# A block-causal attention with a gated MLP on one core: written order in the first slots, weight pieces spread over ten slots, and the softmax sums inverted later

## The chip, the cores and the metric

The kernel runs on one core of a Trainium2 chip. The metric is the device time of one execution in microseconds. Three runs of the kernel before gave 811.85, 812.12 and 814.16 us, so its time is the median, 812.12 us. The engines are PE (TensorE matmul), PEld (its weight loads), DVE (VectorE), ACT (ScalarE), POOL (GpSimd) and SP (which issues DMAs).

## What is computed

```python
scores = scale * np.matmul(q, k.transpose(0, 1, 3, 2))      # 8 batches, 8 heads, S = 576, D = 64, fp32
scores = np.where(block_i >= block_j, scores, -1000000000.0)  # blocks of 64 positions
attn = np.exp(scores - np.max(scores, axis=-1, keepdims=True))
attn = attn / (np.sum(attn, axis=-1, keepdims=True) + 1e-09)
x = np.matmul(attn, v)                                       # heads laid side by side: (8, 576, 512)
h = x @ w_in                                                 # 512 x 1024, float64 in memory
h = 0.5 * h * (1.0 + np.tanh(c * (h + 0.044715 * h ** 3)))
u, v = h[..., :512], h[..., 512:]
v_n = (v - mu) / np.sqrt(var + 1e-06) * g_ln                 # over the 512 features
v_s = np.einsum('ts,bsd->btd', w_sg, v_n) + b_sg[None, :, None]
out = x + (u * v_s) @ w_out                                  # w_out float64 in memory
```

## The kernel before

Every fp32 product is made of three matmuls: each operand is split into a high part (a cast, `xh`, `kh`, `wi_h`) and a low part (a subtraction, `xl`, `kl`, `wi_l`), and high x high, high x low and low x high are summed in PSUM.

The work is cut into 32 **slots** of one pair of heads each, four slots to a batch (`slot`, L647). A slot makes the softmax sums' inverse (`inverse`, L370: DVE writes `r` from `sums` and inverts it, POOL copies it wide into `rx`), transposes the unnormalised probabilities of its own pair in three parts (`turn`, tiles `pA`, `pB`, `pC`, copied to `ptA`, `ptB`, `ptC` by DVE for one head or by ACT for the other), transposes `rx` into the tiles `pd` and `pe` (`turn_sums`), and multiplies with v (`products`, tile `ob`; `normalise` writes `x` and stores it to `spill`). In between it makes the next pair's scores (`first` and `second`, tile `s`), on which DVE finds the ten maxima (L303) and ACT the exponentials (L316). `split_qk` (L96, POOL) splits q and k of the pair after that.

A batch's **feed-forward** is a queue of groups that are put into holes of the slots of the following batch: 5 v groups (`accv`, a copy by ACT, gelu, and the layer norm as `side` work: moments, `rs`, `centre` on DVE, `scale` L517 to L531 with `vv` on POOL, `vh` on DVE, `vl` on POOL), 8 u groups (`accu`), 8 o groups of the batch before it (`acco`, residual page `xr` loaded from `spill`, summed by DVE and stored as `out_T`), and 8 s groups (`accs`, which need all of `vh` and `vl`). `PLAN` says how many groups stand in each of a slot's four holes: "1112" for the first slot of a batch, "2114" for the other three. So slot 4k holds v, 4k+1 u, 4k+2 o and 4k+3 s; the first batch has no o before it, so its s groups already stand in slot 6.

**Weights.** w_in and w_out are float64 and are converted in pieces of 256 columns (`from_f64`, L170): ACT's absolute value, three DVE operations, ACT's cast (`wi_h`), POOL's subtraction (`wi_l`). Spatial weights w_sgT are split by ACT and POOL (`ws_h`, `ws_l`; the last page with a bias row). `WS` says how many pieces a slot converts: 2, 2, 2, 2, 8, 2, 2, 2, 4, 4; `need` (L256) converts at once what is missing when a part begins.

**What sets the order.** Only PE runs in the order in which the program is written (`PIN = "P"`, L50). On DVE, ACT, POOL and SP a scheduler orders the instructions at build time; in each queue they then run one after the other.

**Buffers.** Pages of one tag share a fixed number of buffers (L57). Tag "r" has two: they hold the residual pages `xr` and also the small tile `r` of `inverse` (L372, the same tag). u, gh, gl and the weight pages have twelve.

Of the kernel before, what the change touches and what calls it, by code (L numbers as in the profile page):

```python
# [20 lines left out]
def kernel(  # L21
# [12 lines left out]
    nc = tc.nc  # L34
# [15 lines left out]
    PIN = "P"  # L50
# [17 lines left out]
    def pin(ins, e):  # L68
        return tc.keep_in_program_order(ins) if e in PIN else ins

    def mm(*a, **k):
        return pin(nc.tensor.matmul(*a, **k), "P")  # L72

    def turn(out, in_):
        return pin(nc.tensor.transpose(out, in_, ident), "P")  # L75
# [20 lines left out]
    def split_qk(n):  # L96
        out = []
        for x, t in zip(raw.pop(n), "qk"):
            hi = sp.tile([P, S], F32R, tag=t + "h", name=t + "h", bufs=1)
            lo = sp.tile([P, S], F32R, tag=t + "l", name=t + "l", bufs=1)  # L100
            if n == 0:
                copy("v" if t == "q" else "a", hi, x)
                nc.vector.tensor_tensor(lo, x, hi.bitcast(F32), op=ALU.subtract)
            else:
                copy("g", hi, x)
                nc.gpsimd.tensor_tensor(lo, x, hi.bitcast(F32), op=ALU.subtract)  # L106
# [19 lines left out]
    t = bank("warm")  # L126
    for _ in range(18):
        nc.tensor.transpose(t[:, :P], ident, ident)
# [3 lines left out]
    nc.gpsimd.memset(mask, 0.0)  # L132
    nc.gpsimd.memset(mask[:BLK, MW - BLK :], -8.0e9)
    half = cp.tile([P, NT], F32, name="half")
    nc.gpsimd.memset(half, -0.5)
    stats = cp.tile([P, NT, 2], F32, name="stats")
    nc.gpsimd.memset(stats, 1.0)


    for s in (0, 1):  # L140
        t = cp.tile([P, NT, 2 * D], F32, name=f"v_f{s}")
        nc.gpsimd.memset(t[TAIL:, NT - 1, :], 0.0)
        v_bufs.append(t)
# [22 lines left out]
    def split_weight(x, dh, dl):  # L166
        nc.scalar.copy(dh, x)
        nc.gpsimd.tensor_tensor(dl, x, dh.bitcast(F32), op=ALU.subtract)

    def from_f64(raw, dh, dl):  # L170
# [4 lines left out]
        tm = page(U32, 2 * n, "w")  # L175
# [14 lines left out]
    def load_weight(src, cols, dh, dl):  # L190

        W = 256
        parts = [(c, slice(f, f + W)) for c in range(NC) for f in range(cols.start, cols.stop, W)]
        raws = {}

        def fetch(k):
            if k < len(parts):
                c, fs = parts[k]
                raws[k] = page(src.dtype, W, "w")
                nc.sync.dma_start(raws[k], src[c * P : (c + 1) * P, fs])  # L200

        for k in range(2):
            fetch(k)
        for k, (c, fs) in enumerate(parts):
            fetch(k + 2)
# [3 lines left out]
            else:  # L209
                from_f64(*args)  # L210
            yield True

    def load_spatial():
        nc.sync.dma_start(g_bc, g_ln.unsqueeze(0).broadcast_to([P, DH]))
        t = page(F32, S, "w")
        nc.gpsimd.memset(t[BLK:, :DH], 1.0)
        nc.vector.tensor_copy(vone[BLK:, :], t[BLK:, :DH])
        for j in range(NT - 1):
            t = page(F32, S, "w")
# [5 lines left out]
        t = page(F32, S, "w")  # L225
        for hf in (0, 1):
            nc.sync.dma_start(t[hf * BLK : (hf + 1) * BLK, :], w_sgT[j * P : S, :])
        t2 = page(F32, S, "w")
        nc.gpsimd.memset(t2[BLK:, :], 0.0)
        nc.sync.dma_start(t2[BLK : BLK + 1, :], b_sg.unsqueeze(0))  # L230
        nc.sync.dma_start(t2[96:97, :], b_sg.unsqueeze(0))
        nc.scalar.copy(ws_h[:, j, :], t)
        nc.gpsimd.tensor_tensor(
            ws_l[:BLK, j, :], t[:BLK, :], ws_h[:BLK, j, :].bitcast(F32), op=ALU.subtract
        )
        nc.scalar.copy(ws_l[BLK:, j, :], t2[BLK:, :])
        nc.vector.tensor_tensor(
# [9 lines left out]
            ("o", load_weight(w_out, slice(0, DM), wo_h, wo_l)),  # L247
# [15 lines left out]
    xs = {}  # L263

    class Scores:


        def __init__(self, n):
            self.qh, self.ql, self.kh, self.kl = qk.pop(n)
            self.sm = sp.tile([P, NT, 2], F32, tag="sums", name="sums", bufs=3)  # L270
            nc.gpsimd.memset(self.sm[:, 0, :], 1.0)
# [27 lines left out]
        def maximum(self, a, i, lo, hi):  # L299
# [3 lines left out]
            nc.vector.tensor_tensor_reduce(  # L303
# [10 lines left out]
        def exponent(self, a, i):  # L314
            r, e = slice(0, QN[i]), EXT[i]
            nc.scalar.activation(  # L316
# [33 lines left out]
    class Values:  # L350
# [19 lines left out]
        def inverse(self):  # L370

            r = sp.tile([P, NT * 2], F32, tag="r", name="r", bufs=2)  # L372
            nc.vector.tensor_scalar_add(r, self.sm.rearrange("p i a -> p (i a)"), 1e-9)
            nc.vector.reciprocal(r, r)
            self.rx = sp.tile([P, NT, 2 * D], F32, tag="rx", name="rx", bufs=1)
            nc.gpsimd.tensor_copy(
# [4 lines left out]
        def turn_sums(self):  # L381
# [4 lines left out]
            t, t2 = bank("pd"), bank("pe")  # L386
            for a in (0, 1):
# [42 lines left out]
        def split(self):  # L430
# [7 lines left out]
            nc.gpsimd.tensor_tensor(lo, x, hi[:, :S].bitcast(F32), op=ALU.subtract)
# [34 lines left out]
    def v_part(b, vv, vn, vn_t, u, g_s):  # L473
        need("v")
        x_s = xs[b]
        for st in range(NT):
# [13 lines left out]
            if st < NT - 1:  # L490
                last = nc.scalar.copy(x, acc).ins
            else:
                vt = sp.tile([P, DH], F32, tag="pt", name="vt", bufs=6)
                nc.scalar.copy(vt[:TAIL, :], acc[BLK:, :])
                nc.vector.tensor_tensor(x, acc[:TAIL, :], vt[:TAIL, :], op=ALU.add)
# [3 lines left out]
        def moments(st):  # L499
# [4 lines left out]
            nc.vector.bn_aggr(stats[:rows, st, :], bs[:rows, :])  # L504
# [8 lines left out]
        def inverse_std():  # L513
            nc.gpsimd.tensor_scalar(rs, stats[:, :, 1], 1e-6, None, op0=ALU.add)
            nc.gpsimd.tensor_tensor(rs, rs, half, op=ALU.pow)

        def scale(st):  # L517
# [6 lines left out]
            if st < NT - 1:  # L524
                hi, lo = vn[st] = page(F32R, DH, "vh"), page(F32R, DH, "vl")
                nc.vector.tensor_copy(hi, x)  # L526
                nc.gpsimd.tensor_tensor(lo, x, hi.bitcast(F32), op=ALU.subtract)  # L527
# [16 lines left out]
    def u_part(b, vv, vn, vn_t, u, g_s):  # L544
        need("u")
        x_s = xs.pop(b)
        for fo in range(NC):
            u.append(page(F32, S, "u"))
            fs = slice(fo * P, (fo + 1) * P)
            for th in (0, 1):  # L550
# [12 lines left out]
                last = nc.scalar.copy(u[fo][:, ts], acc[:, :SH]).ins  # L563
# [192 lines left out]
```

## Time and profile before

| what | value |
|---|---|
| median of 3 runs | 812.12 us (811.85 to 814.16) |
| the profiled execution | 813.77 us, span 812.0 us, mean granted clock 0.968 |
| PE busy | 761.3 us (94%), 7090 instructions |
| DVE, ACT, POOL busy | 480.9, 411.4, 397.0 us |
| chain that ended last, by engine | PE 86%, DVE 5%, POOL 3%, DMA 2% |
| longest wait of PE | 14.5 us, `accs` for `vh` |

The span is the time from the first to the last instruction. A row of the trace gives the start, the length, the engine, the line, the operation and its tiles, and in brackets the idle time before it and what ended that. The chain of waits is followed back from the last instruction: at each step to what released it.

### The profile page before, as it was taken

To read this page: it belongs to the slowest core of one execution; us is meant where nothing else is said; L and a number is where in the kernel's file an instruction comes from. 1 tells how busy PE (TensorE), PEld (TensorE's weight loads), DVE (VectorE), ACT (ScalarE), POOL (GpSimd) and SP (SyncE) were. 2 spreads that over 40 slices of the span, in tenths; PEclk is the share of its full clock that TensorE was granted. 3 is DMA by queue.
4 is the path that set the end of the run, shared out by engine and by line. 5 is a ranking of instruction groups with operands and counts; after the bars stand their busy time and mean duration, and the time that the engine had idled before them with its cause. 6 is when DMAs were issued, how large, how long until landed. Compare 5 with 4: busy or idle time off the path is not lost.

```text
span 812.0 us, 18284 instructions
## 1 busy us (share of the span) xinstructions
PE 761.3 (94%) x7090; PEld 714.0 (88%) x7090; DVE 480.9 (59%) x1477; ACT 411.4 (51%) x1061; POOL 397.0 (49%) x457
## 2 busy tenths in 40 slices
PE   4588993699999999999999999999999999999997
PEld 4467893598999989999999989999899989999997
DVE  6975448277596635854486644865477644952542
ACT  5575585056764357533764347624674337630500
POOL 4664338464467522854358423764348423742341
PEclk8699997599999999999999999999999999999999
DMA  7323225023234112321134112321133211320032
GB/s 242 111 87 89 63 73 153 0 72 99 60 104 132 49 41 79 101 88 57 60 89 137 43 57 60 119 87 59 61 89 113 64 36 56 102 88 16 1 117 88
DMA packets 46922, 65.84 MB, mean 81 GB/s; under 512 B 4082, under 2 KB 22514, under 8 KB 46836
## 3 DMA queue, kind: packets, MB, share of 16 engines
q1 hardware_dynamic: 46836, 64.67, 25.8%
q8 instruction: 56, 0.92, 0.5%
q14 instruction: 30, 0.25, 0.1%
HBM read 45.78 MB, written 18.87 MB: 80 GB/s over the span
## 4 chain that ended last, share of the span: by engine, by line
PE 86%; DVE 5%; POOL 3%; DMA 2%; issue 2%; ACT 1%; DVEq 0%; SPq 0%; POOLq 0%
PE accs L72 15%; PE accv L72 13%; PE accu L72 13%; PE acco L72 12%; PE ob L72 10%; PE s L72 10%; PE pC L75 4%; PE pB L75 4%; PE pA L75 3%; PE pd L75 2%; DVE prob L303 1%; DVE w L181 1%; ACT prob L316 1%; PE pe L75 1%; DVE w L182 1%
## 5 line engine op out<-in xcount | busy, mean ns | idle before, releaser
L316 ACT ACTIVATE prob<-prob,negm 128x576 f32<-128x576 f32 (+3 forms) x320 | 176.8, 554 | 86.5 <-DVE negm L303 83.5
L303 DVE CUSTOM_DVE_ANT_0 prob<-s,mask 128x288 f32<-128x288 f32 (+3 forms) x320 | 121.8, 424 | 61.8 <-PE s L72 61.1
L72 PE MATMUL accs<-ws_h,vh 128*128 128x288 f32 x256 | 79.8, 312 | 16.5 <-DVE vh L526 16.5
L596 POOL TENSOR_TENSOR gl<-u,gh 128x288 fp32r<-128x288 f32 x64 | 52.1, 817 | 64.5 <-DVE gh L595 64.2
L435 POOL TENSOR_TENSOR xh<-x,xh 128x64 fp32r<-128x64 f32 x32 | 14.0, 438 | 140.0 <-DVE xh L434 137.6
L72 PE MATMUL accs<-ws_h,vl 128*128 128x288 f32 x256 | 77.5, 303 | 2.8 <-POOL vl L527 2.8
L72 PE MATMUL accu<-xh,wi_h 128*128 128x288 f32 x256 | 78.1, 305 | 0.0
L72 PE MATMUL acco<-gh,wo_h 128*128 128x288 f32 x256 | 77.8, 304 | 0.0
L72 PE MATMUL accs<-ws_l,vh 128*128 128x288 f32 x256 | 76.5, 299 | 0.0
L72 PE MATMUL accu<-xl,wi_h 128*128 128x288 f32 x256 | 75.4, 295 | 0.0
L72 PE MATMUL acco<-gh,wo_l 128*128 128x288 f32 x256 | 75.4, 295 | 0.0
L72 PE MATMUL accu<-xh,wi_l 128*128 128x288 f32 x256 | 75.4, 295 | 0.0
L72 PE MATMUL acco<-gl,wo_h 128*128 128x288 f32 x256 | 75.4, 294 | 0.0
L594 DVE TENSOR_TENSOR u<-accs,u 128x288 f32<-128x288 f32 x64 | 29.3, 458 | 63.9 <-PE accs L72 63.2
L72 PE MATMUL accv<-wi_h,xh 128*128 128x512 f32 x160 | 65.8, 411 | 0.0
L72 PEld LDWEIGHTS accs<-ws_h,vh 128*128 128x128 f32 x256 | 49.1, 192 | 18.9 <-DVE vh L526 15.7
L72 PE MATMUL s<-kh,qh 64*128 64x288 f32 (+4 forms) x384 | 63.3, 324 | 0.0
L72 PE MATMUL accv<-wi_l,xh 128*128 128x512 f32 x160 | 63.2, 395 | 0.0
L79 POOL CAST kh<-k_f 128x576 fp32r<-128x576 f32 x31 | 21.1, 681 | 84.1 <-PE s L72 79.5
L72 PE MATMUL s<-kh,ql 64*128 64x288 f32 (+4 forms) x384 | 59.6, 305 | 0.8 <-POOL ql L106 0.8
L316 ACT ACTIVATION_READ_ACCUMULATOR prob<-prob,negm 128x1 f32 x320 | 59.8, 187 | 0.0
L72 PE MATMUL s<-kl,qh 64*128 64x288 f32 (+4 forms) x384 | 58.4, 302 | 0.0
(118 smaller groups left out, 2163.7 us busy)
## 6 DMA issues: line engine op xcount, KB each, us to landing
q_f<-in_qT SPq DMA_DIRECT2D x32, 288.0 KB, 3.0
k_f<-in_kT SPq DMA_DIRECT2D x32, 288.0 KB, 2.8
spill<-x SPq DMA_DIRECT2D x32, 288.0 KB, 2.7
xr<-spill SPq DMA_DIRECT2D x32, 288.0 KB, 2.9
out_T<-xr SPq DMA_DIRECT2D x32, 288.0 KB, 2.1
v_f<-in_v SPq DMA_DIRECT2D x32, 256.0 KB, 3.0
w<-in_w_in SPq DMA_DIRECT2D x16, 256.0 KB, 4.7
w<-in_w_out SPq DMA_DIRECT2D x8, 256.0 KB, 3.2
```

The lines of the kernel that those rows point to most:

```text
L72: return pin(nc.tensor.matmul(*a, **k), "P")
L75: return pin(nc.tensor.transpose(out, in_, ident), "P")
L79: return f(dst, src)
L181: nc.vector.tensor_scalar(t, lo, 29, None, op0=ALU.logical_shift_right)
L182: nc.vector.scalar_tensor_tensor(t, hi, 0x80000000, t, op0=ALU.bitwise_and, op1=ALU.bitwise_or)
L303: nc.vector.tensor_tensor_reduce(prob[a][i][r, lo:hi], self.where[a, i, lo], mask[r, MW - (hi - lo) :] if 0 < i and hi == e else mask[r, : ...
L316: nc.scalar.activation(prob[a][i][r, :e], prob[a][i][r, :e], AF.Exp, bias=self.negm[a][r, i : i + 1], scale=-1.0, accum_out=self.sm[r, i, ...
L435: nc.gpsimd.tensor_tensor(hi[:, S:], x[:, S - TAIL :], hi[:, S - TAIL : S].bitcast(F32), op=ALU.subtract)
L594: nc.vector.tensor_tensor(x, acc[:, :SH], x, op=ALU.mult)
L596: nc.gpsimd.tensor_tensor(glo[:, ts], x, ghi[:, ts].bitcast(F32), op=ALU.subtract)
```

## The change

- All four engines run in written order while slots 0 to 3 are issued (`written`); from slot 4 on again only PE. The operations that may be pinned go through a wrapper, so their line in the profile is that of the wrapper.
- The four first slots convert two w_in pieces each, after the sums' transposes, taken column block by column block; the remaining pieces stand at the end of slots 4, 6, 7, 8 and 9, from slot 4 on behind the last maximum on DVE and the last exponential on ACT (`issue_after`).
- Spatial and w_out pages move from the tag with twelve buffers to tag "r" with two; w_out pieces are no longer loaded two ahead.
- `inverse` moves, in all 32 slots, from the slot's start to behind turn B.
- The first batch's groups follow `FIRST`: 5, 4, 4 and 8 in slots 4 to 7, so that its s part comes in slot 7.
- 16 transposes more at the start and 8 in each of the first four slots, whose results nobody uses.

```diff
-    PIN = "P"
+    written = set("P")
+    class Engine:
+        def __init__(self, letter, engine):
+            self.letter, self.engine = letter, engine
+        def __getattr__(self, name):
+            method = getattr(self.engine, name)
+            return lambda *a, **k: pin(method(*a, **k), self.letter)
+    vector = Engine("V", nc.vector)
...
-        return tc.keep_in_program_order(ins) if e in PIN else ins
+        return tc.keep_in_program_order(ins) if e in written else ins
...
-    def load_weight(src, cols, dh, dl):
+    def load_weight(src, cols, dh, dl, name="w", ahead=2):
         W = 256
-        parts = [(c, slice(f, f + W)) for c in range(NC) for f in range(cols.start, cols.stop, W)]
+        parts = [(c, slice(f, f + W)) for f in range(cols.start, cols.stop, W) for c in range(NC)]
...
     def load_spatial():
...
-            t = page(F32, S, "w")
+            t = page(F32, S, "xr")
             nc.sync.dma_start(t, w_sgT[j * P : (j + 1) * P, :])
...
-            ("o", load_weight(w_out, slice(0, DM), wo_h, wo_l)),
+            ("o", load_weight(w_out, slice(0, DM), wo_h, wo_l, "xr", 0)),
...
-        def turn_sums(self):
+        def turn_sums(self, idle):
             t, t2 = bank("pd"), bank("pe")
+            warm(t2, idle)
...
-    WS = [2, 2, 2, 2, 8, 2, 2, 2, 4, 4]
+    WS = [(0, 2, 0, 0), (0, 2, 0, 0), (0, 2, 0, 0), (0, 2, 0, 0), (0, 0, 0, 5), (0, 0, 0, 0)]
+    WS += [(0, 0, 0, 5), (0, 0, 0, 2), (0, 0, 0, 3), (0, 0, 0, 3)]
     def load_share(n, k):
         if n < len(WS):
-            for _ in range(WS[n] * (k + 1) // 4 - WS[n] * k // 4):
-                weight_step()
+            with ExitStack() as order:
+                if n >= H // 2:
+                    for ins in behind.values():
+                        order.enter_context(tc.issue_after(ins.ins))
+                for _ in range(WS[n][k]):
+                    weight_step()
     PLAN = ["1112", "2114", "2114", "2114"]
+    FIRST = ["1112", "1111", "1111", "2114"]
     def slot(n, sc):
...
+        if n == q:
+            written.intersection_update("P")
+        g = [int(x) for x in (FIRST if n // q == 1 else PLAN)[n % q]]
...
-        va.inverse()
         va.turn(0, "A")
         va.turn(1, "A")
         hole(g[0])
...
         va.turn(0, "B")
         va.turn(1, "B")
+        va.inverse()
         hole(g[1])
...
-        va.turn_sums()
+        va.turn_sums(8 if n < q else 0)
...
     load_v(0)
+    written.update("VAG")
     split_qk(0)
```

What this moves in the queues, at three places. First **POOL ahead of the first batch's s part**, in before (slot 6; `ws_l` and `wo_l` are low parts of spatial weights and w_out, `vv` the scaled rows, `vl` their low parts):

```order
L514 TENSOR_SCALAR rs<-stats 128x5
L229 MEMSET w 64x576
L168 TENSOR_TENSOR ws_l<-w,ws_h 128x576 x2
L515 TENSOR_TENSOR rs<-rs,half 128x5
L233 TENSOR_TENSOR ws_l<-w,ws_h 64x576
L168 TENSOR_TENSOR wo_l<-w,wo_h 128x256
L522 TENSOR_TENSOR vv<-vv,rs 64x512
L522 TENSOR_TENSOR vv<-vv,rs 128x512
L527 TENSOR_TENSOR vl<-vv,vh 128x512
```

and in after (slot 7):

```order
L60 TENSOR_TENSOR kl<-k_f,kh 128x576
L60 TENSOR_TENSOR ws_l<-xr,ws_h 128x576 x2
L60 TENSOR_TENSOR ql<-q_f,qh 128x576
L60 TENSOR_TENSOR ws_l<-xr,ws_h 128x576
L60 MEMSET xr 64x576
L60 TENSOR_TENSOR ws_l<-xr,ws_h 64x576
L60 TENSOR_TENSOR wo_l<-xr,wo_h 128x256
L541 TENSOR_TENSOR vv<-vv,rs 64x512
L541 TENSOR_TENSOR vv<-vv,rs 128x512
L60 MEMSET sums 128x2
L60 COPY rx<-r 128x640
L60 TENSOR_TENSOR vl<-vv,vh 128x512
```

The `ws_l` and `wo_l` of the weights stand ahead of the `vv` in both; in after the slot's own `kl`, `ql` and the copy `rx` stand among them, and `rs` is already done further up.

Second **DVE in slot 14**, an o slot of the steady state, in before, with `r` among the moments at the slot's start (`bs` and `stats` are the layer norm's):

```order
L504 BN_AGGR stats_99<-bs_4172 128x2
L503 BN_STATS bs_4175<-vv_3718 128x6
L373 TENSOR_SCALAR r_4247<-sums_4043 128x10
L504 BN_AGGR stats_99<-bs_4175 128x2
L503 BN_STATS bs_4178<-vv_3761 128x6
L374 RECIPROCAL r_4247<-r_4247 128x10
L504 BN_AGGR stats_99<-bs_4178 128x2
```

and in after, with `r` behind the third residual sum `xr` (L60 is the wrapper's line; xr_4310 is the first residual page):

```order
L60 CAST vn_t_3697<-vv_3950 64x512
L60 COPY ptB_4376<-pB_4370 128x512
L60 TENSOR_TENSOR vn_t_3697<-vv_3950,vn_t_3697 64x512
L60 CAST vh_4343<-vv_3731 128x512
L60 TENSOR_TENSOR xr_4310<-acco_4383,xr_4310 128x288
L60 COPY ptC_4409<-pC_4403 128x512
L60 TENSOR_SCALAR r_4378<-sums_4092 128x10
L60 CAST vh_4348<-vv_3767 128x512
L60 RECIPROCAL r_4378<-r_4378 128x10
L60 CAST vh_4353<-vv_3810 128x512
L60 CAST vh_4399<-vv_3939 128x512
L60 TENSOR_TENSOR xr_4326<-acco_4431,xr_4326 128x288
```

`r` has moved behind ptA, ptB, ptC, three sums of residual pages and the first `vh`; the second to fourth `vh` now stand behind it.

Third **POOL in slot 14**, in before, where the copy `rx` stands ahead of `ql` and the layer norm:

```order
L376 COPY rx_4250<-r_4247 128x640
L106 TENSOR_TENSOR ql_4150<-q_f_3907,qh_4149 128x576
L435 TENSOR_TENSOR xh_4313<-x_4120,xh_4313 128x64
L438 TENSOR_TENSOR xl_4314<-x_4120,xh_4313 128x576
L514 TENSOR_SCALAR rs_3930<-stats_99 128x5
L515 TENSOR_TENSOR rs_3930<-rs_3930,half_97 128x5
L522 TENSOR_TENSOR vv_3901<-vv_3901,rs_3930 64x512
L522 TENSOR_TENSOR vv_3687<-vv_3687,rs_3930 128x512
```

and in after:

```order
L60 TENSOR_SCALAR rs_3974<-stats_99 128x5
L60 TENSOR_TENSOR rs_3974<-rs_3974,half_97 128x5
L541 TENSOR_TENSOR vv_3950<-vv_3950,rs_3974 64x512
L541 TENSOR_TENSOR vv_3731<-vv_3731,rs_3974 128x512
L60 TENSOR_TENSOR vl_4344<-vv_3731,vh_4343 128x512
L541 TENSOR_TENSOR vv_3767<-vv_3767,rs_3974 128x512
L60 MEMSET sums_5086 128x2
L60 TENSOR_TENSOR vl_4349<-vv_3767,vh_4348 128x512
L541 TENSOR_TENSOR vv_3810<-vv_3810,rs_3974 128x512
L60 COPY rx_4381<-r_4378 128x640
L541 TENSOR_TENSOR vv_3939<-vv_3939,rs_3974 128x512
```

The copy `rx` has moved behind four `vv` (one of them the short tail) and two `vl`.

More of the change, by code (lines that the diff above doesn't have):

```diff
@@ L125, with warm @@
     make_identity(nc, ident)
-    t = bank("warm")
-    for _ in range(18):
-        nc.tensor.transpose(t[:, :P], ident, ident)
+    def warm(t, k):
+        for _ in range(k):
+            turn(t[:, :P], ident)
+    warm(bank("warm"), 18)
     MW = EXT[NT - 2]
     mask = cp.tile([P, MW], BF16, name="mask")
-    nc.gpsimd.memset(mask, 0.0)
-    nc.gpsimd.memset(mask[:BLK, MW - BLK :], -8.0e9)
+    gpsimd.memset(mask, 0.0)
+    gpsimd.memset(mask[:BLK, MW - BLK :], -8.0e9)
     half = cp.tile([P, NT], F32, name="half")
-    nc.gpsimd.memset(half, -0.5)
+    gpsimd.memset(half, -0.5)
     stats = cp.tile([P, NT, 2], F32, name="stats")
-    nc.gpsimd.memset(stats, 1.0)
+    gpsimd.memset(stats, 1.0)
     for s in (0, 1):
         t = cp.tile([P, NT, 2 * D], F32, name=f"v_f{s}")
-        nc.gpsimd.memset(t[TAIL:, NT - 1, :], 0.0)
+        gpsimd.memset(t[TAIL:, NT - 1, :], 0.0)
         v_bufs.append(t)
@@ L198, in fetch @@
                 c, fs = parts[k]
-                raws[k] = page(src.dtype, W, "w")
+                raws[k] = page(src.dtype, W, name)
                 nc.sync.dma_start(raws[k], src[c * P : (c + 1) * P, fs])
-        for k in range(2):
+        for k in range(ahead):
             fetch(k)
         for k, (c, fs) in enumerate(parts):
-            fetch(k + 2)
+            fetch(k + ahead)
             args = (raws.pop(k), dh[:, c, fs], dl[:, c, fs])
@@ L214, in load_spatial @@
         nc.sync.dma_start(g_bc, g_ln.unsqueeze(0).broadcast_to([P, DH]))
-        t = page(F32, S, "w")
-        nc.gpsimd.memset(t[BLK:, :DH], 1.0)
-        nc.vector.tensor_copy(vone[BLK:, :], t[BLK:, :DH])
+        t = page(F32, S, "xr")
+        gpsimd.memset(t[BLK:, :DH], 1.0)
+        vector.tensor_copy(vone[BLK:, :], t[BLK:, :DH])
         for j in range(NT - 1):
-            t = page(F32, S, "w")
+            t = page(F32, S, "xr")
             nc.sync.dma_start(t, w_sgT[j * P : (j + 1) * P, :])
@@ L263 @@
     xs = {}
+    behind = {}
     class Scores:
@@ L315, in exponent @@
             r, e = slice(0, QN[i]), EXT[i]
-            nc.scalar.activation(
+            behind["A"] = scalar.activation(
                 prob[a][i][r, :e],
@@ L490, in v_part @@
             if st < NT - 1:
-                last = nc.scalar.copy(x, acc).ins
+                last = scalar.copy(x, acc).ins
             else:
                 vt = sp.tile([P, DH], F32, tag="pt", name="vt", bufs=6)
-                nc.scalar.copy(vt[:TAIL, :], acc[BLK:, :])
-                nc.vector.tensor_tensor(x, acc[:TAIL, :], vt[:TAIL, :], op=ALU.add)
+                scalar.copy(vt[:TAIL, :], acc[BLK:, :])
+                vector.tensor_tensor(x, acc[:TAIL, :], vt[:TAIL, :], op=ALU.add)
             yield "v"
@@ L513, in inverse_std @@
         def inverse_std():
-            nc.gpsimd.tensor_scalar(rs, stats[:, :, 1], 1e-6, None, op0=ALU.add)
-            nc.gpsimd.tensor_tensor(rs, rs, half, op=ALU.pow)
+            gpsimd.tensor_scalar(rs, stats[:, :, 1], 1e-6, None, op0=ALU.add)
+            gpsimd.tensor_tensor(rs, rs, half, op=ALU.pow)
         def scale(st):
@@ L562, in u_part @@
                         )
-                last = nc.scalar.copy(u[fo][:, ts], acc[:, :SH]).ins
+                last = scalar.copy(u[fo][:, ts], acc[:, :SH]).ins
                 if fo * 2 + th == 2 * NC - 1:
@@ L702 @@
     split_qk(1)
+    warm(bank("warm"), 16)
     for n in range(N):
```

99 lines of the change are left out of this document (51 added, 48 removed).

## The prediction

> **What bounds the kernel now.** I read the page first: its busy time and its slices.
>
> ```profile
> PE 761.3 (94%) x7090; PEld 714.0 (88%) x7090; DVE 480.9 (59%) x1477; ACT 411.4 (51%) x1061; POOL 397.0 (49%) x457
> PE   4588993699999999999999999999999999999997
> PEclk8699997599999999999999999999999999999999
> ```
>
> TensorE is busy for 94% of the span. The loss lies in the first eight slices of 20.3 us; from there to the last slice the digit is 9. So anything that keeps PE waiting after about 160 us is paid in full, and a gain can come only from the start. The stretches by engine say where (columns: length; busy us of PE, PEld, DVE, ACT, POOL; granted clock; DMA share; GB/s):
>
> ```profile
> 130.00:140.00 10.00, 0.00 (x0) 0.00 (x0) 8.70 (x9) 6.58 (x12) 8.92 (x9) 0.61 0.27 90
> 140.00:150.00 10.00, 3.03 (x7) 1.72 (x7) 3.99 (x7) 0.00 (x0) 7.05 (x7) 0.50 0.09 26
> ```
>
> Twenty microseconds hold 3 us of PE work: the first batch's s part waits for the normalised v. In the chain of waits the start reads so (start, length, what):
>
> ```profile
> 48.61 0.72 POOL rx L376
> 49.32 1.38 POOL ql L106
> 50.75 1.52 PE s L72 x22
> 52.27 2.82 PE ob L72 x56
> ...
> 61.24 0.72 POOL rx L376
> ...
> 83.38 1.02 PE pA L75 x8
> ...
> 122.28 6.58 PE accu L72 x48
> ...
> 153.94 4.69 PE accs L72 x18
> ...
> 179.15 0.87 PE pA L75 x8
> ```
>
> Slots 0 to 3 go round a ring of 61.24 - 48.61 = 12.6 us in which PE and POOL take turns. Slot 4 starts at 83.4, slot 6 at 122.28 + 6.58 = 128.9. The last wait of the s part ends at 153.9, 25.1 into slot 6, and slot 7 starts 25.2 after that. In slot 7 no feed-forward group runs, and slot 8 starts at
>
> ```profile
> 188.65 1.09 PE L75 MATMUL pA<-ident,prob 128*128 128x128 f32 x8
> ```
>
> so 188.65 - 179.15 = 9.5 us is the attention of a slot alone. From there on 812.0 - 188.65 = 623.35 us are PE-bound.
>
> **The change, part by part.** *Written order and two weight pieces in slots 0 to 3.* In before, weight conversions stand among the first maxima, and slot 1's rx only ends at 49.3. In after, DVE comes to slot 0's ten maxima at once. From the start of s (50.75) to the end of rx (61.96) the ring needs 11.2, 2.8 of it ob, which slot 0 doesn't have: 8.4. With q and k there and split at about 5, and 1.3 for what the ring hid of the second products, rx of slot 0 ends near 14.7 (13.5 to 16). The ring itself gets no shorter:
>
> ```profile
> L106 POOL TENSOR_TENSOR kl<-k_f,kh 128x576 fp32r<-128x576 f32 x4 | 5.9, 1464 | 0.0
> L438 POOL TENSOR_TENSOR xl<-x,xh 128x576 fp32r<-128x576 f32 x4 | 5.7, 1421 | 0.0
> ```
>
> In written order POOL does both splits of q and k (two casts of about 0.7, two subtractions of 1.46: 4.3), xh and xl of the previous pair (0.3 and 1.42) and rx (0.72): 6.7. PE's part beside it is pd and pe 0.65, s 1.5 and 1.3, ob 2.8 and the first block's 0.3: 6.6. That is 13.4 a slot against 12.6, because ql no longer lies behind rx. rx of slot 3 ends at 14.7 + 3 x 13.4 = 54.9; PE's 6.6 follow, and 3.0 for a u piece's DVE and POOL operations that the written order puts in between and for xl ahead of the v part: slot 4 starts at **64.5**, a gain of 18.9. Bounds: 62.7 (ring 12.8) and 69.5 (PE at the low clock, priced below, in three slots). The warm transposes lie in PE's wait for rx; if that cover is gone, eight of them at a third of pd's 0.49 for three cost 1.3 us a slot.
>
> *Slots 4 to 6, groups 5-4-4-8.* Slots 4 and 5 took 128.9 - 83.4 = 45.5. Four u groups less are -6.6, xl of slot 3 comes 0.8 later, and since the rest of the u pieces is now converted there, on ACT behind the v copies, a table load and gelus, and in a row on POOL, slot 5's u groups wait: 2.7 to 4.2 by my count of those operations, I take 4.1. So 43.8. Slot 6: 9.5 + 6.6 = 16.1. Slot 7 then starts at 64.5 + 43.8 + 16.1 = **124.4**.
>
> *Slot 7, the s part.* Does the longer lead bring the normalised v ahead? POOL's rows in before, and the loads:
>
> ```profile
> 144.21 1.26 POOL L527 TENSOR_TENSOR vl<-vv,vh 128x512 fp32r<-128x512 f32 x1 [1.87 <-DVE vh L526]
> ...
> 152.62 1.27 POOL L527 TENSOR_TENSOR vl<-vv,vh 128x512 fp32r<-128x512 f32 x1 [0.54 <-DVE vh L526]
> ```
> ```profile
> out_T<-xr SPq DMA_DIRECT2D x32, 288.0 KB, 2.1
> ...
> w<-in_w_out SPq DMA_DIRECT2D x8, 256.0 KB, 3.2
> w<-in_w_sgT SPq DMA_DIRECT2D x4, 288.0 KB, 3.7
> ```
>
> In after, all spatial ws_l and the first wo_l stand on POOL ahead of the first vv scale; on DVE the last two centres stand behind the one-row ws_l and the three operations of that w_out piece. And these pages go through two buffers instead of twelve, so loads and conversions follow one another. From slot 7's start: xh and xl of two pairs, kl, two ws_l, ql, at 1.4 to 1.45 each and 0.3 for an xh: to 10.7. The third w_sgT page loads once the first ws_l is through (7.9 + 3.7 = 11.6), is cast and subtracted: 13.7. That buffer's next use is a memset and two bias rows, one after the other, for which I take the 2.1 of out_T: 18.4. Cast and one-row ws_l: about 20.5. The w_out piece (landed by 20): abs, three DVE operations, cast, wo_l: 23 to 25.5. Two centres, two vv scales, rx, the first vl: 28. The last vl follows by 152.62 - 144.21 = 8.4: about **35** (33 to 37), where it was 25.1. The wait is moved by a slot, not removed. After it come the same 25.2 us: 124.4 + 35 + 25.2 = 184.6; I take **184.1** for slot 8 (the first pairs go quicker when vh is ready) **against 188.65: -4.6**. Of 18.9 us gained, 14 are given back here.
>
> *Slot 9.* The last w_out pieces take the buffers and DVE ahead of r: between 0 and 6 by the same durations, I take the middle, **+3.2**.
>
> *r after turn B, in two buffers that the residual pages and the weights share.* In every slot 4k+2 from 10 to 30 the o part runs, and its first two residual pages, x_r0 and x_r1, are now taken before r. r gets x_r0's buffer, so it must wait until x_r0 is stored, after the third o group. Before, r was done at the slot's start. What stands there on PE, POOL and DVE in slots 10 and 11 of before:
>
> ```profile
> 234.34 1.04 PE L75 MATMUL pA<-ident,prob 128*128 128x128 f32 x8
> ...
> 242.39 0.49 PE L75 MATMUL pd<-ident,rx 128*128 128x128 f32 x3
> ```
> ```profile
> 248.69 1.04 POOL L522 TENSOR_TENSOR vv<-vv,rs 128x512 f32<-128x512 f32 x1
> ```
> ```profile
> 241.28 0.46 DVE L620 TENSOR_TENSOR xr<-acco,xr 128x288 f32<-128x288 f32 x1 [0.40 <-PE acco L72]
> ...
> 256.88 0.60 DVE L373 TENSOR_SCALAR r<-sums 128x10 f32<-128x10 f32 x1 [0.98 <-DMA out_T<-xr]
> ```
>
> The last row shows the mechanism already at work: r of slot 11 waits for such a store. pd needs rx 242.39 - 234.34 = 8.05 us after pA. By data alone the third residual sum ends at slot start + 7.3, out_T lands 2.1 later, r and reciprocal take 0.7, rx 0.72: 10.8, 2.7 late. In the new order, moreover, rx stands on POOL behind the second vl and the third vv, and the vh that this vl needs stands on DVE behind r, while vone, vn_t and the first vh stand ahead of the third sum. With slot 10's times: third sum at 243.2 (1.5 later than now), out_T at 245.4, r 246.1, vh 246.5, vl 247.8, vv 248.9, rx 249.65. That is **7.3 late** in each of five slots (14, 18, 22, 26, 30): **36.5**. Bounds 2.7 and 9. In slot 10 the moments, centres and late residual loads stand ahead of r too; by the same steps rx comes at slot start + 18, **+9.9**. Behind pd PE has an o group, the next scores and all products in fixed order, so nothing fills the wait, and PE, bound from there to the end, doesn't catch up.
>
> *The clock.* Waits of this size have a second price:
>
> ```profile
> 33.29 0.90 PE L75 MATMUL pd<-ident,rx 128*128 128x128 f32 x3 [6.60 <-POOL rx L376]
> ...
> 36.32 0.44 PE L72 MATMUL s<-kh,ql 64*128 64x288 f32 x2
> ```
>
> After 6.6 us of idle PE, three transposes take 0.90 instead of 0.49, and the slow pace lasts to about 36.6: 3.3 us at half speed, 1.65 lost. I take 2 for each of six waits: **12**. The ends are 0 and 19; the upper is 3.1 a wait, if the slow time is 6.3 as it may be after longer waits.
>
> The Trainium skill, "TensorE: Matmul & The Clock Gate", Part 1 on the clock gate, says that one idle window of about 3.4 us halves the clock and that about 3.4 us of sustained work restores it. By that rule each wait would add an estimated 1.7 us, six of them 10, and the sum would be 867; the trace agrees (3.3 us slow after the idle 6.6).
>
> **The sum.** Against the profiled execution (span 812.0, own time 813.77): -4.6 + 3.2 + 9.9 + 36.5 + 12 = +57.0, so a span of 869.0 and an own time of 870.8. The profiled execution is 1.65 above the median of the runs, 812.12; on that the forecast is **869**.
>
> **The rivals.**
>
> *Only the data path delays rx, and the clock holds*: POOL and DVE are free when out_T lands. Six waits of 2.7: 812.1 - 4.6 + 16.2 = 824. For: POOL no longer has the early rx copy ahead of its vl and vv. Against: vh and vl stand between in any case, which alone makes it 5.
>
> *Slot 7's wait is gone.* The v part ends a slot earlier than the s part needs it, and the scales could be through in slot 6. Then slot 7 takes at most the 25.2 that follow the wait: 869 - 35 = 834. Against: POOL's order, wo_l ahead of the first vv. It decides at the last vl done within 1 us of slot 7's start.
>
> *rx is in time* (the other side). If r still gets its buffer ahead of x_r0, or out_T and rx are through by slot start + 8.05 in slots 9, 10, 14 and on, the 3.2, 9.9, 36.5 and 12 all go: 812.1 - 4.6 = 807.5, faster. One mechanism, price 61.6, turning point 8.05. For: PE has work up to then, and 58 of its 61.6 us rest on r's place alone. Against: 2.1 us of out_T and 1.4 of r and rx do not fit between the sum at 7.3 and pd at 8.05.
>
> *Both of the last two:* 807.5 - 35 = 772.
>
> *The change does less than it says in the first slots* (PE at the low clock there): slot 4 at 69.5 and the whole 5 later, 874, inside the forecast's range.
>
> **How the numbers follow.** Forecast 0.66, data path alone 0.10, slot 7 free 0.08, rx in time 0.07, both 0.06; 0.03 for a balance within 0.3%, which is about what a measurement of this kernel can tell from no change (its runs spread from 811.85 to 814.16). Faster by more than that: 0.07 + 0.06 and 0.01 of the data path case with a shorter slot 7, 0.14. Slower: 0.83. The low end is the data path case, 823. The high end is 9 instead of 7.3 in five waits (+8.5), 3.1 of clock each (+6.6), slots 9 and 4 near their bounds (+6): 890. Outside lie the 0.16 of faster and same below, and a few hundredths above.
>
> **What would show it.** Right: pA of slot 4 near 64.5; PE's accs waiting on vh and vl in slot 7 until near 159; pd waiting on rx for 5 to 10 us in slots 10, 14 and on, r itself waiting on the DMA out_T; dents in PE's slices and in its clock after slice 9. Wrong: pd without a wait in slot 14; accs without a wait in slot 7; slots 0 to 3 longer than 15 us each.

## The result and the profile after

The changed kernel takes 871.2 us (median of 4 runs, 870.15 to 871.57), the kernel before 812.0 beside it (811.77 to 814.16): 1.072 times the time before, interval 1.070 to 1.074. The forecast was 869. The profiled execution of the changed kernel took 871.45 with a span of 869.7.

The slices of PE and of its clock, from the page of the changed kernel (a slice is 21.7 us now):

```profile
PE   9889980799869999799969999699996999799998
PEclk9999895699979999799989999799997999999999
```

The first five slices have gained: 9889 and 9 where 45889 stood. The hole of the s part stays (0 and 7, clock 5 and 6). New are dents in PE and its clock, every 102 us, to the end. PE's longest waits name both (us in all, times, longest), in the kernel before and in the changed one:

```profile
PE accs L72 <- DVE vh L526: 16.5, 4, 14.5
PE pd L75 <- POOL rx L376: 10.0, 4, 6.6
```
```profile
PE pd L60 <- POOL rx L60: 50.0, 10, 8.2
PE accs L60 <- DVE vh L60: 25.8, 4, 23.6
```

So pd's wait for rx rose from 10.0 to 50.0 us and that of accs from 16.5 to 25.8. By the starts of the slots (pA) the difference comes together so:

| stretch | before | after | difference | forecast |
|---|---|---|---|---|
| start of slot 4 | 83.3 | 64.0 | -19.3 | -18.9 |
| start of slot 7 | 179.0 | 126.9 | | 124.4 |
| start of slot 8 | 188.7 | 186.6 | -2.1 | -4.6 |
| slot 9 | 22.5 | 25.45 | +2.95 | +3.2 |
| slot 10 | 22.5 | 33.1 | +10.6 | +11.9 |
| slots 14, 18, 22, 26, 30 together | 112.5 | 160.0 | +47.5 | +46.5 |
| all others and the tail | | | -1.2 | 0 |
| span | 812.0 | 869.7 | +57.7 | +57.0 |

(The forecast of slots 10 to 30 holds 2 us of low clock for each.) The chain of waits of the changed kernel in slot 14, which starts at 337.9:

```profile
346.45 0.43 DVE vh L60
346.88 0.38 DVE xr L60
347.25 0.02 issue
347.27 2.12 DMA out_T<-xr
...
349.51 0.18 DVE r L60
...
350.09 1.26 POOL vl L60
351.35 1.00 POOL vv L541
352.35 0.67 POOL rx L60
353.02 0.04 issue
353.07 0.90 PE pd L60 x3
```

It is the forecast's chain link by link: third residual sum, store, r, the second vl, a vv, rx, pd, 15.2 after the slot's start where 8.05 is free of waits. PE's own rows show wait and clock:

```profile
353.07 0.90 PE L60 MATMUL pd<-ident,rx 128*128 128x128 f32 x3 [6.95 <-POOL rx L60]
...
356.83 0.44 PE L60 MATMUL acco<-gh,wo_l 128*128 128x288 f32 x1
...
358.77 0.29 PE L60 MATMUL s<-kh,ql 64*128 64x288 f32 x2
```

After 6.95 us of idle PE a matmul takes 0.44 until about 358.5, 0.29 after: 5.4 us at half speed (granted clock 0.5), 2.7 lost. Slots 14 to 26 lost 9.6 to 9.9 each: the wait of 6.9 and 2.7 to 3.0 for the slow clock. Slot 30 lost 8.4. Slot 7's chain shows what replaced the wait of slot 6:

```profile
132.12 1.38 POOL ws_l L60
133.51 3.23 DMA xr<-in_w_sgT
...
141.04 2.72 DMA xr<-in_w_out
...
145.75 1.32 POOL wo_l L60
147.07 1.00 POOL vv L541
...
161.23 4.69 PE accs L60 x18
```

Two loads stand bare in it, since a page must be used up before the next can be loaded. The last wait ends 34.3 after the slot's start; 35 was forecast.

### The profile page after: what moved, and what is told of

Read it like the earlier page. It is cut to its first block, busy times and chain, and to the rows that moved or that the text cites. A ratio compares the mean times of both kernels' runs of the same rounds, so it can differ in the third digit from the quotient of the medians.

```text
span 869.7 us, 18395 instructions
## 1 busy us (share of the span) xinstructions
PE 778.7 (90%) x7138; PEld 730.5 (84%) x7138; DVE 493.2 (57%) x1477; ACT 410.5 (47%) x1061; POOL 393.2 (45%) x457
## 4 chain that ended last, share of the span: by engine, by line
PE 75%; POOL 11%; DVE 6%; DMA 3%; ACT 3%; issue 1%; DVEq 0%; POOLq 0%; SPq 0%; ACTq 0%
PE accs L60 14%; PE accu L60 11%; PE accv L60 10%; PE s L60 10%; PE ob L60 10%; PE acco L60 9%; PE pB L60 3%; PE pC L60 3%; PE pd L60 2%; POOL xl L60 2%; POOL vv L541 2%; PE pA L60 2%; PE pe L60 1%; POOL vl L60 1%; POOL rs L60 1%
## 5 line engine op out<-in xcount | busy, mean ns | idle before, releaser
L60 ACT ACTIVATE prob<-prob,negm 128x576 f32<-128x576 f32 (+3 forms) x320 | 176.5, 553 | 85.4 <-DVE negm L60 82.0
L60 DVE CUSTOM_DVE_ANT_0 prob<-s,mask 128x288 f32<-128x288 f32 (+3 forms) x320 | 121.4, 424 | 62.9 <-PE s L60 62.2
L60 PE MATMUL accs<-ws_h,vh 128*128 128x288 f32 x256 | 79.7, 311 | 25.8 <-DVE vh L60 25.8
L60 POOL TENSOR_TENSOR xh<-x,xh 128x64 fp32r<-128x64 f32 x32 | 13.0, 406 | 169.6 <-DVE xh L60 160.1
L60 POOL TENSOR_TENSOR gl<-u,gh 128x288 fp32r<-128x288 f32 x64 | 52.2, 819 | 78.8 <-DVE gh L60 78.5
L60 PE MATMUL acco<-gh,wo_h 128*128 128x288 f32 x256 | 81.5, 318 | 0.0
L60 PE MATMUL accu<-xh,wi_h 128*128 128x288 f32 x256 | 79.5, 311 | 2.1 <-ACT wi_h L60 2.1
L60 PE MATMUL accs<-ws_h,vl 128*128 128x288 f32 x256 | 77.5, 303 | 2.7 <-POOL vl L60 2.7
L60 PE MATMUL acco<-gl,wo_h 128*128 128x288 f32 x256 | 78.7, 307 | 0.0
L60 PE MATMUL acco<-gh,wo_l 128*128 128x288 f32 x256 | 78.6, 307 | 0.0
L60 PE MATMUL accs<-ws_l,vh 128*128 128x288 f32 x256 | 76.5, 299 | 0.0
L60 PE MATMUL accu<-xh,wi_l 128*128 128x288 f32 x256 | 76.5, 299 | 0.0
L60 PE MATMUL accu<-xl,wi_h 128*128 128x288 f32 x256 | 76.2, 298 | 0.0
L60 PEld LDWEIGHTS accs<-ws_h,vh 128*128 128x128 f32 x256 | 49.1, 192 | 28.1 <-issue 26.9
L60 DVE TENSOR_TENSOR u<-accs,u 128x288 f32<-128x288 f32 x64 | 29.3, 457 | 65.6 <-PE accs L60 65.0
L60 PE MATMUL accv<-wi_h,xh 128*128 128x512 f32 x160 | 65.8, 411 | 0.0
L60 PE MATMUL s<-kh,qh 64*128 64x288 f32 (+4 forms) x384 | 64.4, 332 | 0.0
L60 PE MATMUL accv<-wi_l,xh 128*128 128x512 f32 x160 | 63.2, 395 | 0.0
L60 PE MATMUL pd<-ident,rx 128*128 128x128 f32 x96 | 18.4, 306 | 50.0 <-POOL rx L60 50.0
L60 POOL CAST kh<-k_f 128x576 fp32r<-128x576 f32 x31 | 20.9, 675 | 88.6 <-PE s L60 72.6
L60 PE MATMUL s<-kh,ql 64*128 64x288 f32 (+4 forms) x384 | 59.8, 308 | 0.0
L60 ACT ACTIVATION_READ_ACCUMULATOR prob<-prob,negm 128x1 f32 x320 | 59.8, 187 | 0.0
```

Of the source, the lines that this page charges most:

```text
L60: return lambda *a, **k: pin(method(*a, **k), self.letter)
```

## The experiments

My theory: r, allocated behind turn B, gets the buffer of the first residual page and so waits for that page's store; PE loses the wait and the low clock after it, in six slots. The start's gain is given back in slot 7, which waits for weights that come late through two buffers. Rivals: the written place of r, or POOL's queue, rather than the buffer; something other than the clock behind the 2.7 us; the spread of the groups. (Each run gives its median, and in brackets its ratio to the kernel before and the interval of that ratio.)

**1. The sums inverted at the slot's start again** (from slot 4 on).

```diff
+        if n >= q:
+            va.inverse()
         va.turn(0, "A")
...
-        va.inverse()
+        if n < q:
+            va.inverse()
```

> The changed kernel with one part undone: from slot 4 on the sums are inverted at the slot's start again; all else as changed. My theory (r behind turn B takes the residual page's buffer and comes late): pd waits for rx in slot 9 and in all six o slots go, and with them 2.7 us of low clock each, 60.7 us in all; the s part's wait in slot 7 stays, slot 8 still starts near 187. About 811 us. Rival, the two shared buffers are the cost wherever r is written, since weights and residual pages also queue in them: 840 us or more, waits of pd stay. Rival, the waits of the start decide: no more than 10 us better, 860.

822.1 us (ratio 1.0107, 1.0082 to 1.0133). All o slots from 14 on are back at 22.5, and slot 8 starts at 185.5 as expected. But 11 us more than expected are left, and they lie in slots 9, 10 and 11: 26.8, 23.6 and 32.2 where before had 22.5, 22.5 and 24.65, 13 us. PE's waits in slot 11 of this run:

```profile
PE accs L60 <- POOL vl L60: 4.3, 2, 4.0
```

The w_out pieces of slots 8 and 9 hold up the second batch's layer norm, and its s part waits in slot 11 (in run 8, which converts them earlier, slots 9 to 11 lose nothing). Slot 9's wait of pd did not go, against the expectation: it is 2.60, after 2.73 in the changed kernel. In both, r stands there on DVE behind a w_out piece that waits 2.5 to 2.6 us for its load, and starts 9.6 to 9.7 us into the slot; in run 2, with buffers of its own, it starts ahead of the slot. In that one slot the first rival is right. In the changed kernel slot 11 took 24.65: slot 10's long wait had given the layer norm the time. So the r waits hid 10 us of another loss.

**2. Buffers of its own for r, its place unchanged.**

```diff
-            r = sp.tile([P, NT * 2], F32, tag="r", name="r", bufs=2)
+            r = sp.tile([P, NT * 2], F32, tag="ri", name="r", bufs=2)
```

> The changed kernel with only r's buffers changed: r gets a tag of its own with two buffers, and stays written behind turn B. My theory (the wait is for the buffer, and the build-time scheduler puts r early where nothing holds it): no wait of pd for rx in the o slots, about 811 us. Rival, the written place alone makes rx late on DVE and POOL: most of the seven waits stay, 850 to 870 us.

826.6 us (1.0168, 1.0143 to 1.0192). No wait of pd from slot 8 on: the theory holds, and the written place alone costs nothing, since r then runs early: in the o slots it starts 3.5 us ahead of the slot's start, as in the kernel before, and not 11.6 behind it, as in the changed one. Two other losses are new or bare: slot 11 takes 36.3 (32.2 in run 1), and slot 0 is 5 us late, because a spatial page now has a free buffer from the start. The chain of this run:

```profile
7.65 6.67 DMA xr<-in_w_sgT
14.32 0.02 issue
14.34 0.03 ACT ws_h L60
```

ACT's cast of that page stands among slot 0's exponentials and waits for its load.

**3. The kernel before with r behind turn B from slot 8 on, and nothing else.**

```diff
-        va.inverse()
+        if n < 8:
+            va.inverse()
         va.turn(0, "A")
...
         va.turn(1, "B")
+        if n >= 8:
+            va.inverse()
```

> The kernel before with one part of the change alone: from slot 8 on the sums are inverted behind turn B, in the shared tag as it was; weights, groups and the first slots as before. My theory: the six o slots from 10 to 30 each take 32 us instead of 22.5, pd waits about 7 us for rx in each and PE's clock halves for some 3 to 5 us after it: 812 + 58 = 870 us. Rival, the late r costs only together with the weight pages in the same buffers or the pinned start: under 825 us.

868.1 us (1.0686, 1.0663 to 1.0709). The o slots take 31.9, 32.2, 32.3, 32.4, 32.4 and 30.9, with pd waits of 6.9 in each, and r starts 11.6 us into each of them, as in the changed kernel. Moving the inverse alone, without any of the other parts, costs 56 us.

**4. PE kept busy in the wait.**

```diff
-        va.turn_sums(8 if n < q else 0)
+        va.turn_sums(8 if n < q else 48 if n % q == 2 and n > 2 * q else 0)
```

> The changed kernel with 48 unused transposes put ahead of pd in the slots 10, 14, 18, 22, 26 and 30; they take some 5.3 us at full clock, less than the 7 us for which PE stands there. My theory (the slots lose 9.6 to 9.9 us of which 7 are the wait and 2.7 the low clock after it): the wait shrinks to under 2 us, the clock holds, about 15 us are won: 856 us. Rival, the 2.7 us are not the clock but work pushed behind the wait: 870 us, no change. Rival, extra PE work only adds: 880 us or more.

859.2 us (1.0578, 1.0556 to 1.06), 12 us better than the changed kernel although PE does more; 15 were expected. The slots 14, 18, 22 and 30 take 29.6 to 29.7, the 22.5 and the wait of 7 alone; pd's remaining wait there is 1.7, and its three transposes take 0.55. In slots 10 (3.06 idle, 33.7 in all) and 26 (2.15, 31.7) the clock still fell, and slot 10 gained nothing. Where the clock held, the 2.7 us are gone: they are the clock.

**5. Spatial weights in twelve buffers** (with r's own buffers, as in 2).

```diff
-            t = page(F32, S, "xr")
+            t = page(F32, S, "w")
             nc.sync.dma_start(t, w_sgT[j * P : (j + 1) * P, :])
```

> The changed kernel with r in buffers of its own and the spatial weights' pages back in the tag with twelve buffers; w_out stays in two. My theory (in slot 7 the two buffers make loads and conversions follow one another: the trace of the changed kernel shows two loads of 3.2 and 2.7 us alone in the chain there): slot 7 takes some 50 us instead of 59.7, slot 8 starts near 177. Rival, the order on POOL and DVE (low parts of the weights ahead of the scaled rows) sets the end whatever the buffers: slot 7 stays at 57 or more.

816.0 us (1.0039, 1.0025 to 1.0054). Slot 7 takes 53.3, between the two. Run 2, which differs in these pages alone, has 58.7 there: their buffers are 5.4 us of the wait, less than the 10 expected. That the rest is the order on POOL and DVE is argued, not tested: w_out still goes through two buffers here. Slot 8 starts at 180.1; slot 11 still takes 36.0.

**6. The first batch's groups 5, 8, 8 again** (on run 1).

```diff
-        g = [int(x) for x in (FIRST if n // q == 1 else PLAN)[n % q]]
+        g = [int(x) for x in PLAN[n % q]]
```

> The kernel of the first run (sums inverted at the slot's start from slot 4 on) with the first batch's groups as before, 5, 8 and 8 in slots 4 to 6, so that the s part stands in slot 6 again. My theory (the spread 5-4-4-8 moves the s part's wait by a slot without shortening it, since the normalised v hangs on the weights' conversions, which are issued a slot later too): slot 8 starts near 176 instead of 185.5, the whole near 812 us. Rival, the spread hides work that is bare without it: slot 8 at 190 or later, 826 us or more.

820.9 us (1.0097, 1.0078 to 1.0116), as fast as run 1. My numbers fail: slot 8 starts at 197.4. The s part is done by 171.0, earlier, but in slot 7 pd then waits 12.8 for rx, behind three wo_l on POOL. In exchange slots 9 to 11 lose nothing. The spread gains 12 us at slot 8 and has lost 11 of them by slot 12.

**7. The copy rx on DVE in the six o slots.**

```diff
-            gpsimd.tensor_copy(
+            copy = (vector if self.n >= 8 and self.n % 4 == 2 else gpsimd).tensor_copy
+            copy(
```

> The changed kernel with the wide copy rx made by DVE right behind the reciprocal in the slots 10, 14, 18, 22, 26 and 30; elsewhere by POOL. My theory (of the 7 us that pd waits, some 4.4 are the way over the residual page's store and DVE's queue, and 2.6 the vv and vl that stand ahead of rx on POOL): the wait falls to some 4.4 us in each, 871 - 16 = 855 us; the low clock stays. Rival, POOL has nothing to do with it: 871. Rival, the store is nothing and POOL all: the wait falls under 1 us, 815 us.

866.1 us (1.0658, 1.0643 to 1.0674): the waits are 6.5 instead of 6.9, not 4.4. Part of the 5 us is not the wait but a shorter slow clock: slots 14 and 26 lose 1.6 behind the wait here, where 2.7 and 3.0 were lost. DVE's rows of this run in slot 14:

```profile
349.04 0.17 DVE L60 TENSOR_SCALAR r<-sums 128x10 f32<-128x10 f32 x1 [1.67 <-DMA out_T<-xr]
349.12 0.42 DVE L60 CAST vh<-vv 128x512 fp32r<-128x512 f32 x1
349.45 0.21 DVE L60 RECIPROCAL r<-r 128x10 f32<-128x10 f32 x1
349.69 1.53 DVE L60 COPY rx<-r 128x640 f32<-128x640 f32 x1
```

DVE needs 1.53 us for the copy that POOL makes in 0.72, which eats part of what leaving POOL's queue saves; the rest of the wait, to 349.0, is the store and what stands ahead of the third sum. The run does not separate POOL's share cleanly; in the changed kernel it is the 2.15 us between the reciprocal's end (350.14) and rx (352.29).

**8. r's own buffers, early r, early weights.** Runs 1, 2 and 5 together, and the spatial pieces a slot earlier, w_out pieces in slots 7 and 8.

```diff
-    WS = [(0, 2, 0, 0), (0, 2, 0, 0), (0, 2, 0, 0), (0, 2, 0, 0), (0, 0, 0, 5), (0, 0, 0, 0)]
-    WS += [(0, 0, 0, 5), (0, 0, 0, 2), (0, 0, 0, 3), (0, 0, 0, 3)]
+    WS = [(0, 2, 0, 0), (0, 2, 0, 0), (0, 2, 0, 0), (0, 2, 0, 0), (0, 0, 0, 5), (0, 0, 0, 4)]
+    WS += [(0, 0, 0, 0), (0, 0, 0, 4), (0, 0, 0, 4), (0, 0, 0, 0)]
```

> Written order in the first four slots and the groups 5-4-4-8 kept; r in buffers of its own and inverted at the slot's start from slot 4 on; spatial weights in the tag with twelve buffers and at the end of slot 5 instead of slot 6; w_out pieces at the end of slots 7 and 8, four each, none in slot 9. My theory (the start's gain of 19 us at slot 4 was lost to the late spatial weights in slot 7, the r waits, and w_out pieces that delay the second batch's layer norm in slots 9 to 11): slot 7 takes 30 to 35 us, slot 8 starts at 155 to 162, slots 9 to 11 as before: 780 to 788 us. Rival, the normalised v is late by itself: slot 7 stays above 45, 800 us or more.

802.5 us (0.9873, 0.9858 to 0.9888), 1.3% below the kernel before, but not the 780 to 788 expected; slot 8 starts at 180.0, not 155 to 162. Slots 9 to 11 are as before (22.5, 22.5, 24.6): that part holds. Slot 7 takes 45.6, the rival's number, and slot 4 starts at 70.7, with a w_out page's conversion among slot 0's exponentials. DVE's row of r in slot 7, which stands ahead of the last two vh, and POOL's rows beside it:

```profile
142.85 4.26 DVE L60 TENSOR_SCALAR r<-sums 128x10 f32<-128x10 f32 x1
```
```profile
142.57 1.25 POOL L541 TENSOR_TENSOR vv<-vv,rs 64x512 f32<-64x512 f32 x1
143.78 0.31 POOL L60 TENSOR_TENSOR xh<-x,xh 128x64 fp32r<-128x64 f32 x1
144.06 1.39 POOL L60 TENSOR_TENSOR xl<-x,xh 128x576 fp32r<-128x576 f32 x1
145.42 0.31 POOL L60 TENSOR_TENSOR xh<-x,xh 128x64 fp32r<-128x64 f32 x1
145.69 1.39 POOL L60 TENSOR_TENSOR xl<-x,xh 128x576 fp32r<-128x576 f32 x1
```

An instruction on ten columns, 0.17 us as a rule, lasts 4.26: it ends when POOL's five instructions in a row do. Run 11 repeats it: 4.27, ended with the same five. It reads as DVE held up by POOL itself. (The expectation of run 12 put this time down to a wait for the exponentials, but the last of these is done at 138.9.)

**9. No written order on DVE, ACT and POOL** (on run 1).

```diff
-    written.update("VAG")
```

> The kernel of the first run (sums inverted at the slot's start from slot 4 on) without the written order on DVE, ACT and POOL in slots 0 to 3; two weight pieces a slot, groups and warm transposes as changed. My theory (the written order is what keeps weight conversions from standing among slot 0's maxima): slot 0's rx comes at 20 or later instead of 15.6 and slot 4 starts at 70 to 80 instead of 64. Rival, the smaller number of pieces in the first slots does it alone: slot 4 at 63 to 65, the whole at 822 as in the first run.

829.7 us (1.021, 1.0185 to 1.0236). pd of slot 0 comes at 29.0 instead of 15.5, slot 4 at 75.0 instead of 63.9. Of the 11 us, 7.6 arrive at the end. The written order carries more than half of the start's gain of 19. The other 8 belong to what else changed in the first slots; no run takes them apart. The likeliest part is the weights: in the kernel before, the scheduler has all 16 w_in pieces converted by 41.3, those meant for slot 4 too, while in this run nine are through by 30 and the rest come from 101 on. (The rival's "smaller number of pieces" is this holding back; `WS` gives two a slot to the first four slots in both kernels.)

**10. No warm transposes** (on run 1): 16 and 8 a slot become none.

```diff
-            warm(t2, idle)
```

> The kernel of the first run without the 48 unused transposes of slots 0 to 3. My theory (they only fill PE's wait for rx, which stays under 3 us without them, so the clock holds): slot 4 starts at 63.5 to 65, the whole within 2 us of 822. Rival, without them the clock halves after each wait as after the 6.6 us wait of slot 0 before: slot 4 at 67 or later, 825 us or more.

822.3 us (1.0126, 1.0098 to 1.0154), as run 1 within the measurement. But the profiled execution, at 826.8, has slot 4 at 68.4, and the three others 822.2 to 822.4. In the profiled one two of PE's waits for rx are 3.46, not under 3 as expected, and the clock fell in each of the slots 1 to 3, behind waits of 2.31, 3.46 and 3.46. The row of slot 2:

```profile
43.71 0.90 PE L60 MATMUL pd<-ident,rx 128*128 128x128 f32 x3 [3.46 <-POOL rx L60]
```

That the others kept the clock there is likely from their times, but they have no profile; whether the warm transposes are worth their place stays open.

**11. As 8, but r shares the two buffers in slots 0 to 3.**

```diff
-            r = sp.tile([P, NT * 2], F32, tag="ri", name="r", bufs=2)
+            r = sp.tile([P, NT * 2], F32, tag="r" if self.n < 4 else "ri", name="r", bufs=2)
```

> The eighth run's kernel, but r shares the two buffers with the residual pages in slots 0 to 3, as changed, and has buffers of its own only from slot 4 on. In the eighth run a w_out page had a free buffer from the start and its conversion stood among slot 0's exponentials: slot 0 came 4.3 us late and slot 4 at 70.7. My theory: slot 4 at 64 again, the rest as in the eighth run: 796 us. Rival, the 6.5 us are absorbed by the wait in slot 7, which ends by its own chain: 802 us, no gain.

796.1 us (0.9791, 0.9771 to 0.9811): slot 4 at 64.8, slot 8 at 173.7, 15 us ahead of before, and nothing lost behind it. This is 75 us faster than the changed kernel.

**12. The layer norm's steps issued earlier** (on 11).

```diff
-        run_side(3)
+        run_side(8 if n in (5, 6) else 3)
```

> The kernel of the run beside it, with the layer norm's steps issued eight at a time instead of three in slots 5 and 6, so that all centres stand ahead of slot 7's maxima and the sums r of slot 7 behind two of the vh. My theory (in the eighth run the last two centres, then r waiting 4.2 us for the exponentials, held the last vh): slot 7's wait of some 13 us shrinks to under 6, slot 7 takes 35 to 38 us instead of 45.6: 787 us. Rival, POOL's vv and vl are the chain and DVE isn't: no more than 2 us better than the run beside it.

796.2 us (0.9793, 0.9774 to 0.9812), no better. PE's waits of run 11, then of this one:

```profile
PE accs L60 <- DVE vh L60: 12.4, 3, 9.7
...
PE accs L60 <- POOL vl L60: 3.5, 3, 1.4
```
```profile
PE accs L60 <- POOL vl L60: 8.6, 4, 3.8
PE accs L60 <- DVE vh L60: 4.8, 4, 2.4
```

r takes no more than 1.05 us in any slot of this run, and the wait for DVE falls by 7.6, but that for POOL rises by 5.1: POOL's vv and vl, between the splits of q, k and x, are the next chain. The rival is right here.

## Why the prediction was right

- *Slots 0 to 3.* rx of slot 0 ended at 15.5 (14.7 said) and the ring took 13.57 (13.4, though its parts add up to 13.3), slot 4 came at 64.0 (64.5). That the last is so close is luck: rx of slot 3 ended 1.3 late, at 56.2, and what follows it took 7.8 where 9.6 were put down. Run 9 shows that the written order is 11 us of the 19.
- *Slots 4 to 6.* Slots 4 and 5 took 46.8 where 43.8 was said, and slot 6 16.1, as said. Three sizes were off here. Slot 4 lost 2.0 (0.8 said), 1.2 of it waits for probabilities, `xl` and `kl`. Slot 5's wait for the u weights was 2.1 (4.1 said). And I had priced that as a wait alone: the clock was at 0.50 for 6.8 us from 92.28 on, some 3.4 lost. In run 4, where it held there after the same wait, the two slots take 45.3, so the clock cost between 1.5 and 3.4. The chain of the changed kernel has the same ten transposes in slot 5 and in slot 6:

```profile
95.49 2.13 PE pB L60 x10
...
113.36 1.09 PE pB L60 x10
```

- *Slot 7.* The last wait ended at slot start + 34.3 (35). The wait was moved, not removed. The number is closer than its sum: 28 for the first vl and 8.4 to the last add up to 36.4, and the rows give 25.9 and 8.4. Of the reasons given, the two buffers are shown for the spatial pages, 5.4 us (run 5). Runs 8 and 11 take 14 us off slot 7, but with those buffers, an earlier r and earlier weights together, so the shares of order and date stay open.
- *Slot 9.* The mechanism is as said, r behind the w_out pieces, and run 2 has no wait there. That +2.95 met +3.2 is luck, for 3.2 was the middle of 0 to 6.
- *r in the shared buffers.* Runs 2 and 3 show it from both sides: without the sharing no wait is left, and the move alone makes all of it in the kernel before. The waits were 6.9 (7.3 said) and 8.2 in slot 10 (9.9 said). The rival with the data path alone said 2.7: POOL and DVE were not free when the store had landed, though run 7 does not tell their shares.
- *The clock.* It cost 2.7 to 3.0 a wait in four slots, 2.4 in slot 10 and 1.5 in slot 30, where 2 was said; run 4 shows that it is the clock.
- *The total.* Its errors cancel: the six waits came to 42.9 (46.4 said), their slow clock to 15.2 (12), slot 8 started 2.5 later than said, and the rest gave back 1.2 that no term holds. The terms and their causes are right; that the sum is within 1 us of the measured 57.7 is luck.
- *The rivals.* "rx in time" was run 1, and gave 822 rather than 807.5: that rival's sum was wrong, because it took slots 9 to 11 as free once r was early. The forecast didn't see this loss of 13 us either, and didn't need to, since the r waits covered it. "Slot 7's wait gone" is not reached by any run; the best, run 12, leaves 44.2 of 59.7.

## What to carry to other kernels

When a small tile shares a rotating pool of buffers with large ones, moving its allocation past theirs makes it wait for their last reader, here a store; give it a tag of its own before moving it. Price a wait of PE by the wait and by the clock after it. And when a wait has been found, ask what it hides: taking the late r away here uncovered 10 us of another loss in slots 10 and 11.

## What the runs showed of the hardware

PE's clock fell after idle times of 3.06 us (run 4), 3.46 (run 10) and 6.9. After shorter ones it did either: in the changed kernel three transposes behind 2.73 us of idle took 0.55, and the clock held; in run 7 the same three behind 2.62 us took 0.89; in run 1 they took 0.55 behind 2.60, and the clock fell 1.4 us later.

```profile
220.32 0.55 PE L60 MATMUL pd<-ident,rx 128*128 128x128 f32 x3 [2.73 <-POOL rx L60]
```
```profile
217.67 0.89 PE L60 MATMUL pd<-ident,rx 128*128 128x128 f32 x3 [2.62 <-POOL rx L60]
```

The traces' record of the granted clock says why the length of the wait does not decide. In all fourteen traces the clock changes only at points that lie whole multiples of 3.41 us apart. Cut along these points, the changed kernel's slot 14 reads so (the columns are the stretch, its length, PE's busy time and the number of its matmuls, the granted clock, the DMA share and the GB/s moved):

```profile
344.87:348.28 3.41, 1.25 (x12) 1.00 0.05 18
348.28:351.69 3.41, 0.00 (x0) 0.50 0.18 69
351.69:355.11 3.42, 2.04 (x9) 0.50 0.29 73
355.11:358.52 3.41, 3.41 (x22) 0.50 0.04 14
358.52:361.93 3.41, 3.41 (x68) 1.00 0.48 159
```

and the stretch of slot 9 that holds most of its wait, with the one behind it:

```profile
218.57:221.99 3.42, 1.67 (x13) 1.00 0.18 54
221.99:225.40 3.41, 3.41 (x54) 1.00 0.08 28
```

The first stretch of slot 14 has 2.16 us of idle, and the next one is slow; 1.75 in slot 9 did not do it. Over the fourteen traces, a stretch at full clock with more than 1.94 us of idle was always followed by a slow one, and one with less than 1.16 never; in between it went both ways, and what decides there stays open. So it matters how a wait lies across these points, for the fall and for the time lost behind it: in slot 14 three slow stretches reach 5.4 us past the wait of 6.95, in slot 30 two reach 2.8 past one of 6.91. The Trainium skill, "TensorE: Matmul & The Clock Gate", Part 1 on the clock gate, says that the window of activity is about 3.4 us and runs freely, without regard to the kernel. The traces agree, with 3.41; but where that page speaks of an idle window, one with 2.16 us of idle was enough here.

Run 8's r, 4.26 us beside five POOL instructions, is the second thing I had not expected. The Trainium skill, "SBUF — State Buffer", section "SBUF: two separate sides", says that GpSimd and some VectorE operations share one pair of ports as an exclusive lock: whichever starts first has it for the whole instruction, and the other is blocked. The rows agree, as far as they go (no run shows whether r used these ports), and show more: r, begun 0.28 us behind the first of five POOL instructions that followed one another without a gap, ended with the last.

A copy of 128x640 that spreads one value over 64 columns took DVE 1.53 us and POOL 0.72.
